# One of eight Wout pieces converted inside the last feed-forward instead of beside the experts

## The chip, the cores and the metric

The kernel runs on one core of one Trainium2 chip. The metric is the device time of one execution in microseconds (us). TensorE is written PE, VectorE DVE, ScalarE ACT, GpSimd POOL and the engine that issues most transfers SP.

## The reference, cut to what matters

```python
x = attention(q, k, v, bias from w1, b1, w2)      # 4 x 8 heads, 576 positions, 64 wide -> 2304 rows x 512
e = argmax(logits of 8 experts); gate = prob[e]   # per row
x = gate * (relu(x @ w1[e]) @ w2[e])              # 512 -> 1024 -> 512, one expert per row
h = x @ w_in                                      # 512 -> 2048
out = relu(h) ** 2 @ w_out                        # 2048 -> 512
```

`w_in` and `w_out` of the last feed-forward come as 64-bit floats. The kernel turns each into a pair of f16 tensors, a high part and the rest that it leaves, and forms a product as three f16 matmuls (high by high, high by rest, rest by high).

## The kernel before, in words

Three stages follow each other, and each overlaps the next at its edges.

**Attention and routing** fill the first 380 us. The change touches nothing there.

**The experts** follow. The rows are sorted into slots of 128 rows of one expert; `run_slots` (L1305) does 22 of them. A slot's PE work is `ff1` (L1222, 96 matmuls of 128 columns) and `ff2` (L1239, 24 matmuls of 512 columns), with a transposition of a later slot between. Where the expert changes, SP loads 2 MB of w1 (`load_slot`, into the tiles that the trace calls kst and wr) and four parts of 512 KB of already converted w2 (`load_w2`, L1019, `vt<-wsc` in the trace). The w2 parts of slot t+1 are asked for inside `ff2(t)`, each as soon as PE has finished with the part that it overwrites. SP issues in the order of the program and waits in that order.

Beside the experts the kernel converts the weights of the last feed-forward: eight pieces of Win, then eight pieces of Wout, 1 MB each (`convert`, L1112). One piece is: a load; on ACT the absolute value of the high words (L1127); on DVE a maximum, a shift with a mask and two bit operations that put a 32-bit float together (L1129 to L1134); for Wout four differences on POOL (L1147), since the last product is done with 7 block products out of 8; on ACT the high part (L1151); on DVE the rest (L1153); and, for Wout, a store of 896 KB to a scratch tensor `wosc` in DRAM (L1155). `pieces` (L1158) cuts all this into calls of a generator, 7 for each piece after the first two, so that neighbouring pieces interleave, and `piece(t, n)` (L1300) is called four times a slot (n = 0 after the first half of `ff1`, 1 before `ff2`, 2 and 3 right behind `ff2`). It advances the generator while fewer than 1 + (t - 2 + 0.25 n) * CPACE calls are done.

**The last feed-forward** (from L1394) goes over 9 blocks of 256 rows. First SP loads the eight Wout pieces back from `wosc` into `woh` (L1528). A block has eight units, `g_unit(j, c)` (L1425): 24 matmuls into a PSUM tile `pf` of which there are four; ACT applies relu into `gf` (L1440). At every odd c the square of the pair of units is taken (L1445 on ACT in blocks 0 and 1), POOL forms four sums (L1450), and `g_split` (L1454) then converts the pair *before* that one: a cast on ACT into the high part (L1457), a subtraction on DVE into the rest (L1458). There are two `gf` tiles, one for each pair in flight. The second matmul (`ff2_of`, L1461) is seven products of 24 matmuls (L1472). Each runs through the eight pieces c of `woh` in order, so piece 7 comes in the last three of the 24, and pair 3 of the block in the last six. The products of block j stand between the units of block j+1: from c = 5 on in block 1, from c = 3 on later. So 13 units run before the first product. `y_split` (L1414) makes f16 pairs of the next block's input rows in a tile `ysr` of its own (two of them), from which DMA transposes read.

Of the kernel before, what the change touches and what calls it, by code (L numbers as in the profile page):

```python
# [7 lines left out]
F32 = mybir.dt.float32  # L8
F16 = mybir.dt.float16
U32 = mybir.dt.uint32  # L10
I32 = mybir.dt.int32
AF = mybir.ActivationFunctionType
ALU = mybir.AluOpType
# [7 lines left out]
NT, DM = B * S, H * D  # L21
E, F1 = 8, 1024
F2 = 2048
P = 128
# [15 lines left out]
W1S, W2S, YS = 64.0, 64.0, 2.0 ** -8  # L40
WIS, RS, WOS = 64.0, 2.0 ** -8, 64.0
OUTS = 2.0 ** -22
CPACE = 6.1
NCONV, NWIN = 16, 8
HSW = 134
TINY64, HUGE = 2.0 ** -15 * 1.125, 3e38

# [37 lines left out]
def body(ctx: ExitStack, tc: tile.TileContext, q, k, v, wsm, emb, tau, mw1, mw2, win, wout, cst_d, lsk_d, ids_d, out):  # L85
    nc = tc.nc
    win, wout = win.bitcast(U32), wout.bitcast(U32)
    PE, ACT, DVE, POOL, SP = nc.tensor, nc.scalar, nc.vector, nc.gpsimd, nc.sync
# [18 lines left out]
    us_t = [cp.tile([P, XX], F32, name=f"us{i}") for i in range(4)]  # L107
# [850 lines left out]
    with tc.manual_schedule():  # L958
# [235 lines left out]
        wrp = ep("e_wr", 1)  # L1194
# [78 lines left out]
                DVE.tensor_copy(orow[:, i:i + 1], yr[:, DM + 1:XW])  # L1273


        conv = pieces([convert(i, wrp) for i in range(NCONV)])
        done = [0]
        state = ["tail"]
        yq, yd = [], []
# [115 lines left out]
        with ExitStack() as fctx:  # L1395
            fp = lambda n, bufs, **kw: tp(fctx, n, bufs, **(kw if "space" in kw else dict(side="right")))
            woh = fp("f_wo", 1).tile([P, 8, 2, 7, 256], F16, name="woh")
            gp = fp("f_g", 2)
            gfp = fp("f_gf", 2)
            op_ = fp("f_o", 2)  # L1400
            up = fp("f_u", 1)
            ysp2 = fp("f_ys", 2)
            pf1 = fp("f_p1", 4, space=PSUM)
            pf2 = fp("f_p2", 1, space=PSUM)
            NB = NTILE // 2
# [8 lines left out]
            def y_split(t):  # L1414
                y2, yr = yv(t // 2), us_t[t % 4]
                y_rows(t, yr)
                ysr = ysp2.tile([P, 2, 4, P], F16, name="ysr")
                y4 = yr[:, :DM].rearrange("p (k n) -> p k n", k=4)
                o = slice(t % 2 * P, t % 2 * P + P)
                ACT.copy(ysr[:, 0], y4)  # L1420
                DVE.tensor_tensor(out=ysr[:, 1], in0=y4, in1=ysr[:, 0], op=ALU.subtract)
                for a in range(2):
                    SP.dma_start_transpose(out=y2[:, a, :, o], in_=ysr[:, a].rearrange("p k n -> p (k n)"))

            def g_unit(j, c):  # L1425
                y2 = yv(j)
                if c == 0:
                    gts[j] = gp.tile([P, 2, 7, 8, P], F16, name="g2")
                p_ = pf1.tile([P, 2, 256], F32, name="pf1")
                for h in range(2):  # L1430
                    f, i = 8 * h + c, 0
                    for kc in range(4):
                        for a, b in ((0, 0), (0, 1), (1, 0)):
                            PE.matmul(p_[:, h], lhsT=wih[:, a, kc, f * P:(f + 1) * P], rhs=y2[:, b, kc, :],  # L1434
                                      start=(i == 0), stop=(i == 11))
                            i += 1
                if c % 2 == 0:
                    gfs[j] = gfp.tile([P, 8, 2, P], F32, name="gf")
                g = gfs[j]
                ACT.activation(g[:, 0:4, c % 2, :], p_.rearrange("p h (i n) -> p (h i) n", i=2), AF.Relu, scale=RS)  # L1440
                if c % 2 == 0:
                    return
                g4 = g[:, 0:4].rearrange("p q c n -> p (q c n)")
                if j < 2:
                    ACT.activation(g4, g4, AF.Square)  # L1445
                else:
                    DVE.tensor_tensor(out=g4, in0=g4, in1=g4, op=ALU.mult)  # L1447
                for d, x, y, op in ((4, 0, 2, ALU.add), (5, 4, 1, ALU.subtract), (6, 1, 0, ALU.subtract),
                                    (7, 3, 5, ALU.subtract)):
                    POOL.tensor_tensor(out=g[:, d], in0=g[:, x], in1=g[:, y], op=op)  # L1450
                g_split()
                late.append((g, gts[j], c - 1))

            def g_split():  # L1454
                while late:
                    g, gt, c = late.pop()
                    ACT.copy(gt[:, 0, :, c:c + 2, :], g[:, 1:8])  # L1457
                    DVE.tensor_tensor(out=gt[:, 1, :, c:c + 2, :], in0=g[:, 1:8], in1=gt[:, 0, :, c:c + 2, :], op=ALU.subtract)  # L1458

            def ff2_of(j):  # L1460
                gt = gts.pop(j)  # L1461
                m = [meta[:, 2 * j + i, 0:1] for i in range(2)]
                bank = [pf2.tile([P, 512], F32, name=f"pf2_{x}")[:, :256] for x in "abcd"]
                pa, pb, pc, pd = bank
                o = [op_.tile([P, DM], F32, name=f"o{i}") for i in range(2)]
                u = lambda nm: up.tile([P, 256], F32, name=nm)

                def prod(ps, s, w, first, end):
                    i = 0
                    for c in range(8):  # L1470
                        for a, b in ((0, 0), (0, 1), (1, 0)):
                            PE.matmul(ps, lhsT=gt[:, a, s, c, :], rhs=woh[:, c, b, w, :],  # L1472
                                      start=(i == 0 and first), stop=(i == 23 and end), skip_group_check=True)
                            i += 1

                def comb(dst, ps, i, x):
                    DVE.scalar_tensor_tensor(out=dst, in0=ps, scalar=m[i], in1=x, op0=ALU.mult, op1=ALU.add)  # L1477

                def put(i, ns=None):
                    t = 2 * j + i  # L1480
                    if t * P >= ZROW:
                        ch, b = TILES[t]
                        r0 = b * S + ch * P
                        for n in (0, 1) if ns is None else (ns,):
                            w = SP.dma_start(out=out[r0:r0 + P, 256 * n:256 * n + 256], in_=o[i][:, 256 * n:256 * n + 256]).ins
                            for other in outs:
                                tc.declare_no_dep(w, other, reason="disjoint rows")
                        return
                    if ns == 1:
                        return  # L1490
                    w = POOL.indirect_dma_start(out=out, out_offset=bass.IndirectOffsetOnAxis(ap=orow[:, t:t + 1], axis=0),
                                                in_=o[i], in_offset=None, bounds_check=NT - 1, oob_is_err=False).ins
                    for other in outs:
                        tc.declare_no_dep(w, other, reason="disjoint rows")
                    outs.append(w)

                prod(pa, 0, 0, True, False)
                s = [u(f"s{i}") for i in range(2)]
                for i in range(2):
                    ACT.activation(s[i], pa, AF.Copy, scale=m[i])  # L1500
                yield
                prod(pb, 4, 4, True, True)
                u2 = [u(f"u{i}") for i in range(2)]
                for i in range(2):
                    comb(u2[i], pb, i, s[i])
                yield
                prod(pc, 3, 3, True, False)
                u4 = u("u4")
                comb(u4, pc, 0, u2[0])
                yield  # L1510
                prod(pd, 5, 5, True, False)
                comb(o[0][:, 256:], pd, 0, u4)
                put(0, 1)
                yield
                prod(pa, 2, 2, False, True)
                ACT.activation(o[1][:, :256], pa, AF.Copy, scale=m[1])  # L1516
                yield
                prod(pc, 6, 1, False, True)
                comb(o[1][:, 256:], pc, 1, u2[1])
                put(1)  # L1520
                yield
                prod(pd, 1, 6, False, True)
                comb(o[0][:, :256], pd, 0, u2[0])
                put(0, 0)
                yield

            for g in range(8):
                SP.dma_start(out=woh[:, g].rearrange("p a q n -> p (a q n)"), in_=wosc[:, g * 3584:(g + 1) * 3584])  # L1528
            for j in range(NB):
                two = ff2_of(j - 1) if j else iter(())  # L1530
                last = j == NB - 1
                for c in range(8):
                    if c > (2 if j > 1 else 4) and not (last and c == 6):
                        next(two, None)
                    g_unit(j, c)
                    if 0 < j < NB - 1:
                        if c == 0:
                            y_load(j + 1)
                        if c in (3, 5):
                            y_split(2 * (j + 1) + c // 2 - 1)  # L1540
                if last:
                    g_split()
                for _ in two:
                    pass
# [68 lines left out]
```

## Time and profile before

| | us |
|---|---|
| median of 3 runs | 1004.47 (1001.83 to 1008.0) |
| the profiled execution | 1002.3 |
| its span, first to last instruction | 1000.4 |
| PE busy in the span | 946.6 (95%) |
| DVE / ACT / POOL busy | 665.8 / 541.6 / 502.7 |
| mean granted TensorE clock | 0.983 of full speed |

A time in the rows is in microseconds from the first instruction, unless it is marked ns. Busy shares are averages over stages with different limits, so the sections below read the stages one by one. "Idle before" is the time in which an engine stood still ahead of a group, with the event that ended most of it.

### The profile page before, as it was taken

The numbers are of one execution on the slowest core, as the hardware profiler recorded it, in microseconds if no ns is written. First come the engines' busy times: TensorE is split into PE (matmuls) and PEld (weight loads), VectorE is DVE, ScalarE is ACT, GpSimd is POOL, SyncE is SP. The second block draws the span as 40 slices with busy tenths as digits, with TensorE's granted clock in tenths as the row PEclk, the third lists the DMA queues.
The fourth block names the chain that finished last, engine by engine and source line by source line (L and its number), as shares of the span: only waits on it lengthen the run. The fifth ranks groups of instructions, "written<-read, shape, count | busy, mean of one in ns | idle before, by whom it ended". The sixth has DMA issues, their size and how long they took to land. (4 is left out here: it accounts for less than half of the span.)

```text
span 1000.4 us, 24973 instructions
## 1 busy us (share of the span) xinstructions
PE 946.6 (95%) x9725; PEld 750.8 (75%) x9725; DVE 665.8 (67%) x1260; ACT 541.6 (54%) x1000; POOL 502.7 (50%) x413
## 2 busy tenths in 40 slices
PE   8687999999899889999899999999999999999998
PEld 5355776677577668777667666688888888888887
DVE  6665999899998774687876987325455546364442
ACT  5576777777777574465665664355233324324231
POOL 1212537447434352466548787476455645454651
PEclk9799999999999989999999999999999999999999
DMA  8989885998779433698898574372111120111101
GB/s 292 318 244 298 292 290 196 277 273 294 222 250 335 155 129 120 236 336 309 330 407 320 196 294 159 119 315 43 33 54 34 36 59 17 49 44 32 33 1 43
DMA packets 79260, 187.18 MB, mean 187 GB/s; under 512 B 26680, under 2 KB 27320, under 8 KB 76544
## 3 DMA queue, kind: packets, MB, share of 16 engines
q1 hardware_dynamic: 73232, 170.50, 50.9%
q0 software_dynamic: 5904, 15.02, 4.4%
q8 instruction: 78, 1.28, 0.6%
q14 instruction: 46, 0.38, 0.1%
HBM read 171.65 MB, written 51.73 MB: 223 GB/s over the span
## 5 line engine op out<-in xcount | busy, mean ns | idle before, releaser
L1450 POOL TENSOR_TENSOR gf<-gf 128x256 f32<-128x256 f32 x144 | 166.1, 1173 | 144.2 <-DVE gf L1447 124.2
L1434 PE MATMUL pf<-big,wih 128*128 128x256 f16 x1728 | 196.0, 273 | 1.0 <-PEq L1388 1.0
L1434 PEld LDWEIGHTS <-wih 128*128 128x128 f16 x1728 | 169.0, 98 | 21.1 <-issue 1.5
L1472 PEld LDWEIGHTS <-g 128*128 128x128 f16 x1512 | 147.4, 98 | 18.7 <-issue 1.0
L1440 ACT ACTIVATE gf<-pf 128x512 f32<-128x512 f32 x72 | 42.3, 596 | 192.1 <-PE pf L1434 144.1
L1231 PE MATMUL ph<-x,w1b 128*128 128x128 f16 x2112 | 125.1, 219 | 2.9 <-ACT x L1215 1.7
L474 POOL TENSOR_TENSOR wh<-wr,w2s_c 128x1024 f16<-128x1024 f32 x32 | 62.3, 1946 | 127.9 <-DMA wr<-in_mw_dram 49.2
L1231 PEld LDWEIGHTS <-w1b 128*128 128x128 f16 x2112 | 120.6, 98 | 7.3 <-issue 1.9
L1246 PE MATMUL py<-vt,h 128*128 128x512 f16 x528 | 119.2, 383 | 5.0 <-DMA vt<-wsc 5.0
L525 ACT ACTIVATE pr<-ssb,mn 128x576 f32<-128x576 f32 x144 | 111.7, 776 | 10.3 <-DVE mn L512 10.2
L1458 DVE TENSOR_TENSOR g<-gf,g 128x1792 f16<-128x1792 f32 x36 | 85.2, 2367 | 46.0 <-ACT g L1457 46.0
L512 DVE CUSTOM_DVE_ANT_0 ssb<-ps_s,bias 128x576 f32<-128x576 f32 x144 | 107.5, 749 | 5.0 <-DMA bias<-bias_d 4.0
L1447 DVE TENSOR_TENSOR gf<-gf 128x1024 f32<-128x1024 f32 x28 | 34.3, 1225 | 114.2 <-ACT gf L1440 114.2
L501 PE MATMUL ps_s<-kst,qd 128*128 128x288 f16 (+1 forms) x640 | 97.1, 292 | 8.6 <-DVE mn L512 5.8
L1246 PEld LDWEIGHTS <-h 128*128 128x128 f16 x528 | 51.2, 99 | 64.0 <-issue 7.7
L534 PE MATMUL ps_t<-cst,pr 128*128 128x128 f32 x576 | 93.6, 286 | 1.4 <-DVE pt L212 1.1
L559 PE MATMUL pv<-pt,vt 128*64 128x128 f32 (+1 forms) x1280 | 85.0, 276 | 6.4 <-DMA vt<-in_v_dram 5.6
L559 PEld LDWEIGHTS pv<-pt,vt 128*64 128x64 f32 x1280 | 67.5, 141 | 22.9 <-issue 16.3
L534 PEld LDWEIGHTS ps_t<-cst,pr 128*128 128x128 f32 x576 | 65.9, 146 | 24.3 <-issue 18.2
L501 PEld LDWEIGHTS <-qd 128*128 128x128 f16 (+1 forms) x640 | 57.0, 102 | 23.6 <-issue 13.3
L1457 ACT CAST g<-gf 128x1792 f16<-128x1792 f32 x36 | 60.3, 1676 | 4.5 <-POOL gf L1450 4.4
L210 ACT COPY pt<-ps_t 128x512 f32<-128x512 f32 x99 | 57.1, 577 | 9.6 <-PE ps_t L534 9.3
(199 smaller groups left out, 1556.9 us busy)
## 6 DMA issues: line engine op xcount, KB each, us to landing
vt<-wsc SPq DMA_DIRECT2D x88, 512.0 KB
wr<-in_mw_dram SPq DMA_DIRECT2D x76, 512.0 KB
kst<-in_mw_dram SPq DMA_DIRECT2D x44, 512.0 KB
wsc<-wh SPq DMA_DIRECT2D x32, 512.0 KB
bias<-bias_d SPq DMA_DIRECT2D x16, 576.0 KB
bias_d<-rt SPq DMA_DIRECT2D x28, 295.5 KB
qd<-qh SPq DMA_DIRECT2D x64, 128.0 KB
wr<-in_win_dram SPq DMA_DIRECT2D x8, 1024.0 KB
```

What stands on the lines that cost most here:

```text
L474: POOL.tensor_tensor(out=wh[:, 0], in0=wr, in1=w2s_c.to_broadcast([P, 1024]), op=ALU.mult)
L501: PE.matmul(s[r, hf, :288], lhsT=qd[:, h2, i, pr, r], rhs=kst[x - x % 2][:, pr, h2, x % 2, js], start=(i == 0), stop=(i == 1))
L512: DVE.tensor_tensor_reduce(out=ss.rearrange("p (a j) -> p a j", a=2), in0=s[:, :, :288], in1=btile[bkey[u]][:, h2].rearrange("p (a j) -> p ...
L525: ACT.activation(pr_sb[k_ // 2][:, h2], ssb.pop(k_), AF.Exp, bias=mns.pop(k_), scale=-1.0, accum_out=sums[c, b][:, h:h + 1])
L534: PE.transpose(pt_ps[k_][:, jc * P:(jc + 1) * P], src[:, j0:j0 + P], eye)
L559: PE.matmul(pv[o, cs], lhsT=vb[:, 2 * jc + h2, d] if jc < 4 else vb[o, 8, d], rhs=a[h2][:, jc, cs] if jc < 4 else e[o, cs], start=(jc == 0 ...
L1231: PE.matmul(p_[:, f4, :], lhsT=w[:, a, kc, f * P:(f + 1) * P], rhs=x2[:, b, kc, :], start=(i == 0), stop=(i == 11))
L1246: PE.matmul(p_, lhsT=h2[:, a, fc, :], rhs=wb2[fc // 2][:, b, fc % 2, :], start=(i == 0), stop=(i == 23))
L1434: PE.matmul(p_[:, h], lhsT=wih[:, a, kc, f * P:(f + 1) * P], rhs=y2[:, b, kc, :], start=(i == 0), stop=(i == 11))
L1450: POOL.tensor_tensor(out=g[:, d], in0=g[:, x], in1=g[:, y], op=op)
L1458: DVE.tensor_tensor(out=gt[:, 1, :, c:c + 2, :], in0=g[:, 1:8], in1=gt[:, 0, :, c:c + 2, :], op=ALU.subtract)
L1472: PE.matmul(ps, lhsT=gt[:, a, s, c, :], rhs=woh[:, c, b, w, :], start=(i == 0 and first), stop=(i == 23 and end), skip_group_check=True)
```

## The change: one piece is left to the last feed-forward

Fifteen pieces are converted beside the experts in place of sixteen, and CPACE goes from 6.1 to 5.75 calls a slot, so that the fewer calls end at the same slot. The last piece (rows 7 of Wout) is loaded by SP at the start of the last feed-forward into a stretch of the second `g2` tile, which is empty until block 1 writes it. Its conversion is the generator `finish`, advanced by one step behind each of the units 3 to 9 (unit 8j + c): 3 the absolute value, 4 the two scalar operations, 5 and 6 the two bit operations, 7 four differences, on DVE now, 8 the high part, 9 the rest. It writes straight into `woh`, with no trip through DRAM. `gf` gets a third tile. The `ysr` tiles go: the f16 pair of input rows t is written over the row buffer that held rows t - 2. The `g2` tile is laid out by pairs.

```diff
-CPACE = 6.1
-NCONV, NWIN = 16, 8
+CPACE = 5.75
+NCONV, NWIN, NLATE = 16, 8, 1
...
-        conv = pieces([convert(i, wrp) for i in range(NCONV)])
+        conv = pieces([convert(i, wrp) for i in range(NCONV - NLATE)])
...
-            gfp = fp("f_gf", 2)
+            gfp = fp("f_gf", 3)
...
-            ysp2 = fp("f_ys", 2)
...
-                ysr = ysp2.tile([P, 2, 4, P], F16, name="ysr")
+                ysr = us_t[(t + 2) % 4][:, :DM].bitcast(F16).rearrange("p (a k n) -> p a k n", a=2, k=4)
...
-                if c == 0:
-                    gts[j] = gp.tile([P, 2, 7, 8, P], F16, name="g2")
+                if c == 0 and j not in gts:
+                    gts[j] = gp.tile([P, 4, 2, 7, 2, P], F16, name="g2")
...
+            for j in range(2):
+                gts[j] = gp.tile([P, 4, 2, 7, 2, P], F16, name="g2")
+            spare = gts[1].rearrange("p d a q c n -> p (d a q c n)").bitcast(U32)
+            rows = [spare[:, :2048], spare[:, 3072:5120]]
+            flat = spare[:, 5120:7168].bitcast(F32)
+            bits = [spare[:, 6144:7168], spare[:, 2048:3072]]
+            for i in range(NLATE):
+                g = 8 - NLATE + i
+                SP.dma_start(out=rows[i], in_=wout[g * P:(g + 1) * P, :])
+
+            def finish(i):
+                wr = rows[i].rearrange("p (n t) -> p n t", t=2)
+                lo, hi = wr[:, :, 0], wr[:, :, 1]
+                tb = flat.rearrange("p (q n) -> p q n", q=8)
+                af, b = flat[:, :1024], bits[i]
+                bf = b.bitcast(F32)
+                ACT.activation(bf, hi.bitcast(F32), AF.Abs)
+                yield
+                DVE.tensor_scalar(bf, bf, TINY64, None, op0=ALU.max)
+                DVE.tensor_scalar(b, b, 3, 0x3FFFFFF8, op0=ALU.logical_shift_left, op1=ALU.bitwise_and)
+                yield
+                DVE.scalar_tensor_tensor(out=b, in0=lo, scalar=29, in1=b, op0=ALU.logical_shift_right, op1=ALU.bitwise_or)
+                yield
+                DVE.scalar_tensor_tensor(out=af.bitcast(U32), in0=hi, scalar=0xC0000000, in1=b,
+                                         op0=ALU.bitwise_and, op1=ALU.bitwise_or)
+                yield
+                for d, x, y in ((4, 0, 1), (5, 2, 4), (6, 2, 0), (7, 3, 5)):
+                    DVE.tensor_tensor(out=tb[:, d], in0=tb[:, x], in1=tb[:, y], op=ALU.subtract)
+                yield
+                dh, dl = (woh[:, 8 - NLATE + i, a].rearrange("p q n -> p (q n)") for a in range(2))
+                ACT.activation(dh, flat[:, 256:], AF.Copy, scale=WOS)
+                yield
+                DVE.scalar_tensor_tensor(out=dl, in0=flat[:, 256:], scalar=WOS, in1=dh, op0=ALU.mult, op1=ALU.subtract)
+                yield
+
+            ends = [finish(i) for i in range(NLATE)]
+            ORDER = {u: (0,) for u in (3, 4, 5, 6, 7, 8, 9)}
+
-            for g in range(8):
+            for g in range(8 - NLATE):
                 SP.dma_start(out=woh[:, g]..., in_=wosc[:, g * 3584:(g + 1) * 3584])
...
                     g_unit(j, c)
+                    for i in ORDER.get(8 * j + c, ()):
+                        next(ends[i])
```

## Rows read from the trace of the kernel before

**Rows 1.** Busy time of each engine in two stretches, experts and last feed-forward.

```profile
core 0: us, PE busy (x) PEld busy (x) DVE busy (x) ACT busy (x) POOL busy (x), PEclk, DMA share, GB/s
380.00:642.00 262.00, 251.42 (x2897) 185.43 (x2898) 191.44 (x308) 146.08 (x186) 165.38 (x143) 0.99 0.72 264
642.00:997.00 355.00, 354.08 (x3240) 316.34 (x3240) 167.35 (x160) 126.67 (x158) 182.82 (x161) 1.00 0.19 60
```

**Rows 2.** Waits of PE from 380 to 642 us: total, times, longest.

```profile
PE py L1246 <- DMA vt<-wsc: 5.0, 3, 3.3
PE ph L1231 <- ACT x L1215: 1.7, 2, 1.0
PE ph L1231 <- DVE w1b L1026: 1.2, 2, 0.6
```

**Rows 3.** Timeline of PE: start, duration, work, count, idle before it and releaser.

```profile
477.79 7.03 PE L1246 MATMUL py<-vt,h 128*128 128x512 f16 x24 [3.32 <-DMA vt<-wsc]
...
490.46 5.34 PE L1246 MATMUL py<-vt,h 128*128 128x512 f16 x24
...
513.79 1.46 PE L1246 MATMUL py<-vt,h 128*128 128x512 f16 x6 [1.20 <-DMA vt<-wsc]
515.75 4.04 PE L1246 MATMUL py<-vt,h 128*128 128x512 f16 x18 [0.51 <-DMA vt<-wsc]
```

**Rows 4.** Timeline of SP: transfers that it issued, in its order.

```profile
460.61 0.34 SPq L1117 DMA_DIRECT2D wr<-in_win_dram  x1
462.56 3.02 SPq L1010 DMA_DIRECT2D kst<-in_mw_dram  x4
...
466.77 5.01 SPq L1019 DMA_DIRECT2D vt<-wsc  x4
...
500.57 0.37 SPq L1120 DMA_DIRECT2D wr<-in_wout_dram  x1
502.93 4.22 SPq L1019 DMA_DIRECT2D vt<-wsc  x4
```

**Rows 5.** Operations of a conversion, and nearest ones: duration ns least/median/most.

```profile
L1127 ACT ACTIVATE tb<-wr x16: 1131/1162/1197, 420.9 to 620.9; 128x1024 f32<-128x1024 f32 x16
L1129 DVE TENSOR_SCALAR tb<-tb x16: 678/684/1126, 422.7 to 625.1; 128x1024 f32<-128x1024 f32 x16
L1132 DVE SCALAR_TENSOR_TENSOR tb<-wr,tb x16: 1210/1222/2057, 424.4 to 626.5; 128x1024 uint32<-128x1024 uint32 x16
L1153 DVE SCALAR_TENSOR_TENSOR wr<-tb,wr x8: 2010/2014/2974, 553.6 to 641.9; 128x1792 f16<-128x1792 f32 x8
L1447 DVE TENSOR_TENSOR gf<-gf x28: 1224/1226/1226, 708.3 to 970.4; 128x1024 f32<-128x1024 f32 x28
```

**Rows 6.** Timeline of the start of the last feed-forward, all engines.

```profile
642.00 23.19 PE L1434 MATMUL pf<-big,wih 128*128 128x256 f16 x211 [1.04 <-PEq L1388]
...
648.06 1.08 ACT L1440 ACTIVATE gf<-pf 128x512 f32<-128x512 f32 x2 [5.75 <-SPq L1388]
...
651.55 4.08 SPq L1528 DMA_DIRECT2D woh<-wosc  x8
651.58 7.55 POOL L1450 TENSOR_TENSOR gf<-gf 128x256 f32<-128x256 f32 x8 [5.89 <-DMA y_d<-ys,yidx]
...
658.64 1.08 ACT L1440 ACTIVATE gf<-pf 128x512 f32<-128x512 f32 x2 [2.44 <-DVE g L1458]
...
660.89 4.68 POOL L1450 TENSOR_TENSOR gf<-gf 128x256 f32<-128x256 f32 x4 [1.76 <-ACT gf L1445]
...
672.65 1.06 ACT L1445 ACTIVATE gf<-gf 128x1024 f32<-128x1024 f32 x1
673.62 1.67 ACT L1457 CAST g<-gf 128x1792 f16<-128x1792 f32 x1
...
675.32 2.57 DVE L1458 TENSOR_TENSOR g<-gf,g 128x1792 f16<-128x1792 f32 x1 [3.87 <-ACT g L1457]
...
676.06 2.78 PE L1472 MATMUL pf_a<-woh,g 128*128 128x256 f16 x24
```

**Rows 7.** Stretches around the end of the loads of woh, columns as in rows 1.

```profile
655.00:672.00 17.00, 17.00 (x158) 15.25 (x156) 7.45 (x3) 9.11 (x10) 13.24 (x12) 1.00 1.01 415
672.00:676.00 4.00, 4.00 (x39) 3.58 (x38) 0.68 (x1) 3.25 (x4) 2.16 (x5) 1.00 0.04 13
```

More of the change, by code (lines that the diff above doesn't have):

```diff
@@ L1456, in g_split @@
                     g, gt, c = late.pop()
-                    ACT.copy(gt[:, 0, :, c:c + 2, :], g[:, 1:8])
-                    DVE.tensor_tensor(out=gt[:, 1, :, c:c + 2, :], in0=g[:, 1:8], in1=gt[:, 0, :, c:c + 2, :], op=ALU.subtract)
+                    ACT.copy(gt[:, c // 2, 0], g[:, 1:8])
+                    DVE.tensor_tensor(out=gt[:, c // 2, 1], in0=g[:, 1:8], in1=gt[:, c // 2, 0], op=ALU.subtract)
             def ff2_of(j):
@@ L1471, in prod @@
                         for a, b in ((0, 0), (0, 1), (1, 0)):
-                            PE.matmul(ps, lhsT=gt[:, a, s, c, :], rhs=woh[:, c, b, w, :],
+                            PE.matmul(ps, lhsT=gt[:, c // 2, a, s, c % 2, :], rhs=woh[:, c, b, w, :],
                                       start=(i == 0 and first), stop=(i == 23 and end), skip_group_check=True)
```

## The prediction

> **What bounds the kernel now.** I first read the busy time by stage. In the last feed-forward PE is busy for 354.08 of 355 us, at full granted clock; in the expert stage for 251.42 of 262 [rows 1]. So PE sets the time in both. Nothing that ACT, DVE or POOL are spared in the last stage can shorten it, and the change takes no matmul away. In the expert stage at most 262 - 251.42 = 10.6 us of idle PE can be won.
>
> Then I read who ends PE's idle time there: 5.0 us wait for converted w2, 1.7 for ACT and 1.2 for DVE [rows 2]. The 5.0 us are one wait of 3.32 us ahead of slot 7's second matmul and two, 1.20 + 0.51, at slot 10's [rows 3]. The first costs more than its idle time: the 24 matmuls behind it took 7.03 us where the same 24 took 5.34 later [rows 3], 1.7 us more. So transfers cost PE 5.0 + 1.7 = 6.7 us at most.
>
> SP's order says what those loads stand behind: slot 7's behind 1 MB of Win and 2 MB of w1, slot 10's behind 1 MB of Wout issued just ahead of it [rows 4].
>
> Last comes the start of the last stage, where the new work lands. Thirteen units run from 642.00 to 676.06, 2.62 us each, and the first product follows without idle time [rows 6].
>
> **Expert stage: the removed piece and the new pace.** A piece's load stands at a fixed call of the generator. Call m runs at the first point with (t - 2 + 0.25n) * CPACE over m - 2.
>
> The load issued at 500.57 is call 45. At 6.1 it is due at 43/6.1 = 7.05, so slot 9, n = 1, ahead of that slot's second matmul and of the w2 loads asked for inside it. At 5.75 it is due at 7.48, so n = 2, behind them. A megabyte at the 415 GB/s of a full queue [rows 7] is 2.5 us, more than the 1.71 us of slot 10's waits, so I let them go: **-1.7** (0 if something else is behind them, and no more than -1.7).
>
> The load issued at 460.61 is call 24: due at 22/6.1 = 3.61 before, (5, n = 3), and at 22/5.75 = 3.83 now, (6, n = 0). There it stands behind the 2 MB of w1 instead of ahead of it. Both stay ahead of slot 7's w2, so the bytes in front are the same. But SP no longer holds the w1 load back, which went out at 462.56, 2 us behind it [rows 4]. Its four issues may start up to 2 us earlier; I take **-1.3** of the 3.32 + 1.7 (ends 0 and -5.0: nearer 0, because the bytes ahead are unchanged).
>
> The rest of the missing piece (its ACT, DVE and POOL work, its 896 KB store) lies beside PE work. The waits for ACT and DVE, 2.9 us together, come from the order of the queues at a few moments, which the pace shifts; I take 0, with -2.9 and +3 as ends. Stage: **-3.0**.
>
> **Last feed-forward: finish.** Prices [rows 5, 6]: absolute value 1.16, two scalar operations 0.68 each (the second priced as the first), two bit operations 1.22 each, high part 1.67 (the cast of the same 1792 columns), rest 2.01. A difference of 256 columns on DVE is not shown. By the line through 1024 columns at 1.226 and 1792 at 2.014 it is 0.44; zero columns' share and a full 1.226 are the ends, so four cost 0.8 to 4.9, and I take 1.7, on the line. DVE gets 7.5 us more, ACT 2.8, POOL nothing, over units 3 to 9, 18.3 us.
>
> What counts is whether it is ready in time. Before, the wait for a free `gf` tile sets the pairs' rhythm (ACT idle 2.44 us until DVE's subtraction ended) [rows 6]. Relu 1.08, square 1.06, cast 1.67 and subtraction 2.57 follow one another, about 6.4 us for a pair against 5.24 on PE. Pair 3's subtraction ends at 675.32 + 2.57 = 677.89, and PE needs it at the 21st matmul of the first product, 676.06 + 20 * 0.109 = 678.24: 0.35 us of slack. The third tile takes that wait away; finish uses up the room again:
>
> - SP can issue the raw piece ahead of the eight loads of 651.55. At 415 GB/s it has landed by about 655.6 (2.5 us and, assumed, 1.5 until ACT may start). ACT is through with pair 0's cast at 658.64 - 2.44 = 656.2 [rows 6], so the absolute value ends at 657.4.
> - DVE: pair 0's subtraction from 656.2 to 658.8, scalar operations to 660.2; pair 1's subtraction to 663.9, the bit operations to 665.2 and 666.4; pair 2's to 669.1, the differences to 670.8.
> - ACT meets the high part right behind unit 8's relu, at 667.1, and stands there until 670.8. Queued behind it are unit 9's relu, pair 4's square and pair 3's cast. The high part ends at 672.5, pair 3's cast at 675.9.
> - DVE: pair 3's subtraction to 678.5, then the rest of piece 7 to 680.5. PE needs that at the 23rd matmul, 676.06 + 22 * 0.109 = 678.46. PE stands for **+2.0**.
>
> The ends: 0 if the differences take 0.8 and the subtractions 2.0 as on an idle DVE; +6 with bit operations at the longest 2.06, differences at 4.9 and a piece that lands 1.5 us later.
>
> Four POOL sums take 3.78 us before DVE works beside them and 4.68 when it does [rows 6]. DVE's two-input operations in finish, 6 us of them, can stretch POOL further, and pair 3's cast waits for POOL. At 6.2 us for four, the chain ends 1.0 us later; this is inside the +6.
>
> The Trainium skill, page "SBUF — State Buffer", section "Who interferes with whom", says that a DVE instruction with two SBUF inputs and a GpSimd instruction that reads SBUF exclude each other for the whole instruction. It speaks against moving the differences to DVE here, and the rows agree in direction (0.9 us more for four). By it alone the sum would be +3.0 for this step in place of +2.0.
>
> **Edits at nothing.** `woh` from seven loads in place of eight, with a raw megabyte ahead: 7.3 MB either way, and before they were in by 672 with nothing needed before 676 [rows 6, 7]. If that cover is gone, PE waits at its first product. `ysr` over the row buffers: the load of the next rows into the same buffer now waits on SP for the transposes that read it, with the next transposes queued behind; each has a block of 39 us (15 groups of 24 matmuls) and is needed only three units into it. The new layout of `g2` changes no operation.
>
> **Sum.** -1.7 - 1.3 + 2.0 = -1.0 on the profiled execution's 1002.3 gives 1001.3. That execution lies 2.2 below the median of the runs, 1004.47. I forecast **1002.5** for the median, half of that distance on top. Chance 0.55.
>
> **Rivals.**
>
> *The waits for w2 all go, and finish fits.* 1002.3 - 6.7 = 995.6. For: 15 pieces leave more room in a queue that was full around both places. Against: slot 7's load keeps 3 MB ahead of it. Chance 0.17.
>
> *Slower: the raw piece lands late.* Seven loads of 896 KB go out right behind it, and these filled the queue until 672 [rows 7]. If all share alike, the piece lands near 671. ACT stands at the absolute value with all relus behind it; PE has only four `pf` tiles, so unit 8, due at 662.96, starts after unit 4's relu at 672.75, 9.8 us late. The chain through finish then ends 6.9 us behind the product's need. 1002.3 - 3.0 + 16.7 = 1016.0. It decides from a landing later than about 661. Against: slot 10's first w2 part was in PE's use 1.96 us ahead of the next one [rows 3], as if transfers complete in order. Chance 0.06. The Trainium skill, page "DMA: Bandwidth & Descriptors", section "Queues, rings and completion order", says that descriptors of one ring are consumed in ring order, though completion is not promised in that order; by it this rival would be smaller still.
>
> *The expert stage only moves its waits.* No gain, another wait like slot 7's (3.3 + 1.7) at a load that now has a piece ahead of it, and +2.0: 1009.3. For: the queue is full there, and several loads change their place in it. Chance 0.14.
>
> *Nothing that PE sees changes*, because the third tile and the freed queues were hidden anyway and finish is in time: 1002.3. Chance 0.08.
>
> **Range and chances.** A measurement of this kernel can tell about 1% (10 us) from no change. The cases lie between 995.6 and 1009.3 but for the late piece; I give **995 to 1010**. Faster by over 1% (below 994.4) needs more than all w2 waits: 0.04. Slower by over 1% (above 1014.5) is the late piece: 0.05. Within: 0.91.
>
> **What would show it.** Right: slot 10's w2 wait gone, slot 7's shorter; units 0 to 12 without idle PE; PE idle some 2 us inside the first product, ended by DVE's rest of piece 7; ACT waiting some 4 us for the differences; no ACT wait for DVE's subtraction in block 0. Wrong: PE idle at unit 8 (the late piece), new w2 waits at other slots, or no idle PE in the first product.

## The result, and the profile after

The changed kernel takes 1018.45 us in the median against 1002.5 for the kernel before, a ratio of 1.0144 (95% interval 1.011 to 1.0177). I had forecast 1002.5 with a range to 1010: it came out slower than the range holds, and slower than before by 11.0 to 17.7 us.

A total alone misleads here. Slot 0's second matmul started anywhere between 395.2 and 414.1 us in the fourteen profiles of this study, though no kernel changes an instruction ahead of it. So I cut each profile at three points: the first `py` (slot 0's second matmul), the first `pf` (first unit) and the first `pf_a` and `pf_b` (first and second product).

| us | before | after | difference |
|---|---|---|---|
| start to slot 0's second matmul | 397.40 | 399.94 | +2.5, spread of the start |
| experts, to the first unit | 244.60 | 250.80 | **+6.2** |
| thirteen units, to the first product | 34.06 | 34.06 | 0 |
| first product, to the second | 5.24 | 10.83 | **+5.6** |
| the rest, to the end of the span | 319.10 | 319.27 | +0.2 |

The change lost 11.8 us of the profile's 14.5 in two places, and the interval of the runs holds that. PE's waits from 380 us to the first unit, as in [rows 2] (total, times, longest):

```profile
PE py L1246 <- DMA vt<-wsc: 4.7, 2, 3.0
PE ph L1231 <- ACT x L1215: 4.3, 3, 2.0
PE px L1214 <- POOL xs L1049: 3.5, 2, 3.0
```

And PE's timeline at these waits and at the first product, as in [rows 3] and [rows 6] (start, duration, work, count, idle before):

```profile
478.65 5.34 PE L1246 MATMUL py<-vt,h 128*128 128x512 f16 x24 [1.65 <-DMA vt<-wsc]
...
514.79 6.85 PE L1246 MATMUL py<-vt,h 128*128 128x512 f16 x24 [3.02 <-DMA vt<-wsc]
...
538.54 0.61 PE L1214 MATMUL px<-eye,xs 128*128 128x128 f16 x4 [3.02 <-POOL xs L1049]
538.95 4.20 PE L1231 MATMUL ph<-x,w1b 128*128 128x128 f16 x48
...
596.59 2.84 PE L1231 MATMUL ph<-x,w1b 128*128 128x128 f16 x48 [1.64 <-ACT x L1215]
...
609.75 4.47 PE L1231 MATMUL ph<-x,w1b 128*128 128x128 f16 x48 [2.01 <-ACT x L1215]
...
650.74 34.22 PE L1433 MATMUL pf<-big,wih 128*128 128x256 f16 x312 [1.51 <-PEq L1388]
684.80 2.35 PE L1471 MATMUL pf_a<-woh,g 128*128 128x256 f16 x20
688.67 0.39 PE L1471 MATMUL pf_a<-woh,g 128*128 128x256 f16 x2 [1.53 <-DVE g L1457]
691.13 0.38 PE L1471 MATMUL pf_a<-woh,g 128*128 128x256 f16 x2 [2.07 <-DVE woh L1558]
691.35 4.45 PE L1433 MATMUL pf<-big,wih 128*128 128x256 f16 x24
695.63 2.78 PE L1471 MATMUL pf_b<-woh,g 128*128 128x256 f16 x24
```

Read the durations beside the idle times. Each wait of 2 us and more here is followed by work that takes 1.4 to 1.7 us too long (6.85 for 5.34, 4.20 and 4.47 for 2.84, 4.45 for 2.78). The granted clock of those stretches says why (PEclk, third column from the right, a mean of full and half clock over the stretch):

```profile
core 0: us, PE busy (x) PEld busy (x) DVE busy (x) ACT busy (x) POOL busy (x), PEclk, DMA share, GB/s
514.80:521.50 6.70, 6.70 (x25) 2.75 (x25) 6.70 (x7) 3.01 (x5) 4.64 (x3) 0.77 1.02 413
539.00:543.00 4.00, 4.00 (x51) 4.00 (x49) 2.39 (x8) 1.73 (x2) 3.22 (x4) 0.65 0.97 386
609.80:614.00 4.20, 4.20 (x48) 4.20 (x48) 2.56 (x4) 1.60 (x3) 3.33 (x4) 0.59 0.68 277
688.60:695.60 7.00, 4.86 (x28) 3.59 (x29) 6.76 (x6) 3.43 (x5) 6.92 (x5) 0.76 0.10 19
```

The first product. Rows of DVE, ACT, POOL and SP there:

```profile
657.64 0.34 SPq L1534 DMA_DIRECT2D g<-in_wout_dram  x1
657.95 2.89 POOL L1449 TENSOR_TENSOR gf<-gf 128x256 f32<-128x256 f32 x4 [5.52 <-ACT gf L1444]
664.58 1.15 ACT L1542 ACTIVATE g<-g 128x1024 f32<-128x1024 f32 x1
668.42 12.09 POOL L1449 TENSOR_TENSOR gf<-gf 128x256 f32<-128x256 f32 x8 [0.55 <-ACT gf L1444]
678.11 3.02 DVE L1553 TENSOR_TENSOR g<-g 128x256 f32<-128x256 f32 x4
681.16 1.70 ACT L1556 ACTIVATE woh<-g 128x1792 f16<-128x1792 f32 x1 [4.53 <-DVE g L1553]
686.04 2.57 DVE L1457 TENSOR_TENSOR g<-gf,g 128x1792 f16<-128x1792 f32 x1 [4.91 <-ACT g L1456]
688.53 2.54 DVE L1558 SCALAR_TENSOR_TENSOR woh<-g,woh 128x1792 f16<-128x1792 f32 x1
```

ACT takes up the absolute value (664.58) without waiting for the raw piece, which SP had issued 6.9 us before. Later it stands 4.53 us for the differences; pair 3's subtraction and the rest of piece 7 come behind one another and end PE's two waits.

### The profile page after: what moved, and what is told of

The parts are those of the page before. It is cut to its first block, busy times and chain, and to the rows that moved or that the text cites. A ratio compares the mean times of both kernels' runs of the same rounds, so it can differ in the third digit from the quotient of the medians.

```text
span 1014.9 us, 24974 instructions
## 1 busy us (share of the span) xinstructions
PE 949.9 (94%) x9725; PEld 752.6 (74%) x9725; DVE 667.6 (66%) x1264; ACT 542.1 (53%) x1000; POOL 495.0 (49%) x409
## 5 line engine op out<-in xcount | busy, mean ns | idle before, releaser
L1449 POOL TENSOR_TENSOR gf<-gf 128x256 f32<-128x256 f32 x144 | 170.8, 1206 | 147.0 <-DVE gf L1446 124.3
L1231 PE MATMUL ph<-x,w1b 128*128 128x128 f16 x2112 | 127.7, 222 | 4.4 <-ACT x L1215 4.3
L1231 PEld LDWEIGHTS <-w1b 128*128 128x128 f16 x2112 | 123.5, 99 | 8.7 <-issue 3.5
```

The costliest lines, as they stand in the source:

```text
L1231: PE.matmul(p_[:, f4, :], lhsT=w[:, a, kc, f * P:(f + 1) * P], rhs=x2[:, b, kc, :], start=(i == 0), stop=(i == 11))
```

## The experiments

Where the loss comes from was cut first by place, then by cause. Stage lengths come from one profile each. The calls of before gave 244.60, 244.72 (e3) and 242.68 (e1), those of the changed kernel 250.80, 250.44 (e2) and 250.79 (e4), and one kernel profiled twice 240.18 and 238.89: a difference of less than 2 us says nothing. Each ratio is to runs of before that were taken beside it; their median was 1002.5 to 1012.5.

| | experts, us | first product, us | ratio to before (95%) |
|---|---|---|---|
| before | 244.60 | 5.24 | 1 |
| after | 250.80 | 10.83 | 1.0144 (1.011 to 1.0177) |
| e1 | 242.68 | 10.46 | 1.0041 (1.0015 to 1.0068) |
| e2 | 250.44 | 5.24 | 1.0039 (1.0002 to 1.0077) |
| e3 | 244.72 | 10.83 | 1.0038 (1.001 to 1.0067) |
| e4 | 250.79 | 5.28 | 1.0059 (1.0023 to 1.0094) |
| e5 | 245.61 | 5.28 | |
| e6 | 240.18 | 5.26 | |
| e7 | 245.34 | 5.28 | 0.999 (0.9963 to 1.0017) |
| e8 | 247.28 | 5.28 | 1.000 (0.9965 to 1.0036) |
| e9 | 238.89 | 5.27 | 0.9968 (0.9935 to 1.0002) |
| e10 | 240.54 | 5.25 | 0.9956 (0.9927 to 0.9985) |
| e11 | 249.29 | 5.24 | 1.0078 (1.0044 to 1.0112) |
| e12 | 239.14 | 5.26 | |

**e1, the last stage's edits alone.**

```diff
-CPACE = 5.75
+CPACE = 6.1
-        conv = pieces([convert(i, wrp) for i in range(NCONV - NLATE)])
+        conv = pieces([convert(i, wrp) for i in range(NCONV)])
```

> All sixteen pieces are converted beside the experts at 6.1 calls a slot, as before, and finish converts piece 7 a second time in the last feed-forward, with its own load and the third gf tile. Theory: the loss has two parts, about 6 us in the expert stage from where the calls fall at the pace of 5.75, and about 5.5 us at the first product of the last stage, where piece 7 comes late. Then this kernel has an expert stage like before (254 us from slot 0's second matmul at 397 to the first unit; within 2 us) and loses 5 to 6 us in the last stage: about 1008. Rival: the expert stage loses because of the edits to the last stage (another layout of its tiles). Then it is near 1016, with the expert stage 6 us longer here too.

The experts took 242.68, no longer than before, and the first product 10.46, with the same two waits of 1.55 and 2.07. The time was 1012.45, above the 1008 of the theory, but before itself stood at 1006.84 beside it; the ratio of 1.0041, or 1.5 to 6.8 us, agrees with -1.9 + 5.2 = 3.3 us. (The 254 us in the expectation is a slip: 642.0 - 397.4 is 244.6.) The new layout of the last stage costs the experts nothing.

**e2, the experts' part alone.**

```diff
-            for i in range(NLATE):
-                g = 8 - NLATE + i
-                SP.dma_start(out=rows[i], in_=wout[g * P:(g + 1) * P, :])
-            ORDER = {u: (0,) for u in (3, 4, 5, 6, 7, 8, 9)}
+            ORDER = {}
-            for g in range(8 - NLATE):
+            for g in range(8):   # piece 7 loaded from wosc's piece 6
```

> Fifteen pieces at 5.75 calls a slot and no finish; the conversion of piece 7 is left out, and woh's piece 7 is loaded from piece 6 in its place. Theory: the expert stage is 6 us longer than before with the same waits as in the changed kernel (x for ACT behind the high part, slot 10's w2, slot 12's xs), and the first product waits for nothing: about 1009. Rival: the expert stage's extra time is chance of that one profile: then 1000 to 1003.

250.44 and 5.24: the two losses are apart, and the expert stage's is no chance of one profile. The ratio, 0.2 to 7.8 us, holds the 5.8 of the stage. Slot 12's wait for xs was 5.1 us here where slots 7 and 10 waited 3.3 for w2 in place of 4.7: what PE gains at those loads it waits for later.

**e3, the pace alone.**

```diff
-CPACE = 5.75
+CPACE = 6.1
```

> The changed kernel with 6.1 calls a slot in place of 5.75, so each call of the fifteen pieces falls where it fell before and the end comes one slot sooner. Theory: the expert stage is like before or up to 2 us shorter, the first product of the last stage still waits 3 to 5 us with the slow clock behind it: 1005 to 1009. Rival: a missing piece costs whatever the pace (by lost spacing between transfers): 1013 to 1018.

244.72, with the waits of before one by one (3.24, 1.22 and 0.50 for w2, 1.04 for x). At this pace the missing piece neither costs nor wins anything that can be told, and the first product is as in the changed kernel. All of the +6.2 comes with the change of pace; whether by the pace itself or by where it puts the calls is for e6 to say. The time, 1009.33, lies just above the forecast, with before at 1006.84 beside it.

**e4, finish one unit shorter.**

```diff
-            ORDER = {u: (0,) for u in (3, 4, 5, 6, 7, 8, 9)}
+            ORDER = {3: (0,), 4: (0, 0), 5: (0,), 6: (0,), 7: (0,), 8: (0,)}
```

> The changed kernel with finish one unit shorter: the first bit operation goes to unit 4, and every later step one unit sooner, the rest of piece 7 at unit 8. Theory: ACT stands at the high part because DVE comes to the differences late; with the steps sooner pair 3's cast no longer waits behind it and piece 7 is ready before it is needed: the first product waits under 0.5 us, the clock stays at full, and the time falls by 4 to 5.5 us, to about 1013. Rival: DVE and POOL holding each other up set the end of the chain, and the order of the steps moves it by less than 1 us: 1017 to 1019.

The first product took 5.28, without a wait. In its timeline the high part and the rest of piece 7 are done 2 us before the product begins:

```profile
670.75 3.44 DVE L1553 TENSOR_TENSOR g<-g 128x256 f32<-128x256 f32 x4
674.11 2.01 DVE L1457 TENSOR_TENSOR g<-gf,g 128x1792 f16<-128x1792 f32 x1
674.22 1.70 ACT L1556 ACTIVATE woh<-g 128x1792 f16<-128x1792 f32 x1 [2.87 <-DVE g L1553]
676.05 2.01 DVE L1558 SCALAR_TENSOR_TENSOR woh<-g,woh 128x1792 f16<-128x1792 f32 x1
...
680.01 2.82 PE L1471 MATMUL pf_a<-woh,g 128*128 128x256 f16 x24
...
685.29 2.78 PE L1471 MATMUL pf_b<-woh,g 128*128 128x256 f16 x24
```

The differences now stand ahead of pair 2's subtraction on DVE (670.75 before 674.11), where in the changed kernel they came behind it (678.11). Counted from the first unit's start they begin 24.8 us after it in place of 27.4, and ACT's high part 28.3 in place of 30.4. The 5.6 us come from the order of finish, not from its work. Pair 3 has no room to spare: its subtraction ends at 682.17, and PE needs it, counted as in the prediction, at 682.19. All kernels below have this order but e11, which has no finish. By the ratios to before the order is worth more than that, 1.0059 against 1.0144, with wide intervals on both.

**e5, without POOL's differences beside the experts** (they are left out there).

```diff
-            for d, x, y, op in ((4, 0, 1, ALU.subtract), (5, 2, 4, ALU.subtract), (6, 2, 0, ALU.subtract),
-                                (7, 3, 5, ALU.subtract)):
-                POOL.tensor_tensor(out=tb[:, d], in0=tb[:, x], in1=tb[:, y], op=op)
```

> The changed kernel with finish one unit sooner, and the four POOL differences of the pieces beside the experts left out, so that ACT's high part there waits only for DVE. Theory: at 5.75 calls a slot ACT meets the high part ahead of the copy of x and stands behind POOL's differences, which is what PE waits for in slots 16 and 17 (1.64 and 2.01 us and a slow clock behind them). Then these waits fall below 1 us together and the expert stage comes down from 250.8 to 245 to 247, with slot 12's wait for xs unchanged, since no difference is formed before it. Rival: DVE's conversions beside the splits of x and w1 are what makes ACT and POOL late: the waits stay within 1 us of 3.65 and the stage at 249 or more.

The stage fell from 250.79 to 245.61, inside the theory's bounds, and PE's waits for x in slots 16 and 17 are gone (a wait for x is counted to the slot in which x is copied; PE stands at the start of the next). The 1.0 that is left lies ahead of slot 0. Slot 12's wait for xs, expected unchanged at 3.0, was 4.7; other profiles of this schedule have 5.1 (e2) and 4.8 (e4).

```profile
PE px L1211 <- POOL xs L1049: 4.7, 1, 4.7
PE py L1243 <- DMA vt<-wsc: 2.4, 2, 1.4
...
PE ph L1228 <- ACT x L1212: 1.0, 1, 1.0
```

In the changed kernel the chain reads: DVE's last bit operation, POOL's differences (behind a scatter that POOL issues from 587.93 to 589.35), ACT's high part, and only then the copy of x.

```profile
586.39 1.33 DVE L1134 SCALAR_TENSOR_TENSOR tb<-wr,tb 128x1024 uint32<-128x1024 uint32 x1 [0.96 <-DVEq L1035]
...
589.38 2.91 POOL L1147 TENSOR_TENSOR tb<-tb 128x256 f32<-128x256 f32 x4
...
592.32 1.70 ACT L1151 ACTIVATE wr<-tb 128x1792 f16<-128x1792 f32 x1 [5.75 <-POOL tb L1147]
...
595.52 1.01 ACT L1215 COPY x<-px 128x1024 f16<-128x1024 f16 x1
```

ACT stands 5.75 us ahead of 592.32 with the relu and the copy of x queued behind. What e5 also takes away is POOL's 2.9 us a piece, so it does not tell ACT's queue from POOL's load. These rows show the chain through ACT's queue; a kernel that only puts the high part behind the copy of x was not run.

**e6, two calls in advance at the same pace.**

```diff
-            while done[0] < (1 if t < 2 else 1 + (t - 2 + 0.25 * n) * CPACE):
+            while done[0] < (1 if t < 2 else 3 + (t - 2 + 0.25 * n) * CPACE):
```

> The changed kernel with finish one unit sooner, still at 5.75 calls a slot, with two calls done in advance: the same work and spacing, each call falls about a third of a slot earlier. Theory: it is the place where a call falls, not the pace or the fewer pieces, that costs 6 us: the waits change place and the expert stage moves by 2 us or more from 250.8, either way. Rival: the pace itself is bad: 250 to 251.5 with waits of the same kind and sum.

240.18: 10.6 us shorter than at the same pace without the advance, and 4.4 shorter than before. So neither the slower pace nor the fewer pieces need cost anything: the 6.2 us depend on where the calls fall.

**e7 and e8, y rows read back early**, at 6.1 and at 5.75.

```diff
-                    if t == 9:
-                        for n in range(4):
-                            SP.dma_start(out=us_t[n][:, :XW], in_=y_d[n * P:(n + 1) * P, :])
+                    if 2 <= t < 6:
+                        SP.dma_start(out=us_t[t - 2][:, :XW], in_=y_d[(t - 2) * P:(t - 1) * P, :])
```

> Fifteen pieces at 6.1 calls a slot, finish one unit sooner, and the first four blocks of y rows read back in slots 2 to 5, one a slot, in place of all four in slot 9. Theory: POOL's scatter of slot 10's rows must wait until the four loads of slot 9 have landed, and they go out into a full queue; that holds POOL for 9.4 us and makes xs late in slot 12. With the loads in slots 2 to 5, where the queue has room, POOL's wait is gone, 1 MB less stands ahead of w2 in slots 10 and 11, and the expert stage falls below 244.6, by 1 to 3 us; the first product takes 5.24. Total 1 to 3 us below before. Rival: POOL's wait is for something else and w2's waits are set by the bytes before slot 9: 244 to 245, total equal to before.

> The same at 5.75 calls a slot. Theory: slot 12's wait for xs (3.02 us in the changed kernel, with 1.4 of slow clock behind it) goes, those for ACT in slots 16 and 17 stay: expert stage 246 to 248. Rival: slot 12's wait comes from DVE conversions beside POOL's work at this pace: 249.5 to 251, with that wait within 1 us of what it was.

In e7 POOL's wait (9.43 us in the changed kernel, 9.25 in the kernel before) ahead of slot 10's scatter was gone (0.17 left), and slot 12's wait with it. But the stage was 245.34, where I expected less than 244.6: the w2 waits stayed at 4.9 us and ran at the slow clock. The theory of POOL's wait held, that of the gain fell, and the time equals that of before, as the rival had it. In e8 slot 12's wait went, the stage fell by 3.5 to 247.28, and the waits for x stayed at slots 16 and 17 (1.64 and 2.03), as the theory had it.

**e9 and e10, the better version.** e9 is the kernel of e6, timed; e10 adds the early y rows.

> The kernel of e6 again (fifteen pieces, 5.75 calls a slot, two calls in advance, finish one unit sooner), timed in rounds against before. Theory: its expert stage of 240.2 against 244.6 repeats within 1 us, the first product takes 5.2, and it is 0.3 to 0.6% faster than before. Rival: that profile was a lucky one: stage 243 or more, no difference that can be measured.

> The kernel of e9 with the first four blocks of y rows read back in slots 2 to 5. Theory: slot 12's last 1.35 us of waiting for xs go and nothing comes in their place: stage 238.5 to 240, 0.4 to 0.7% faster than before. Rival: loads taken from slot 9 come to stand ahead of w2 in slots 5 to 7, and the waits for w2 grow by what slot 12 saves: 240 to 242.

e9's stage came out at 238.89, 1.3 below e6's where I expected 1 at most. Its time is lower by 0.3%, but its interval just touches no change. e10 beats before by 0.44%, interval 0.15 to 0.73%; its stage of 240.54 lies in the rival's range. Slot 12 no longer waits, but slot 10 waits 3.64 us for w2 and its 24 matmuls take 8.16 in place of 5.34, more than what slot 12 saved. So the early rows add nothing that these runs can tell from e9. PE's waits in e9, where nothing is left from slot 13 on:

```profile
PE py L1246 <- DMA vt<-wsc: 4.2, 3, 2.2
PE px L1214 <- POOL xs L1049: 1.6, 1, 1.6
PE ph L1231 <- ACT x L1215: 0.7, 1, 0.7
```

**e11, the advance without the change.** The line of e6, in the kernel before.

> The kernel before (sixteen pieces at 6.1, all beside the experts) with two calls in advance, as in e6. Theory: what e6 wins comes from where the calls fall and is to be had without moving a piece: the expert stage changes by 2 us or more from 244.6, and if it falls to 241 the moved piece is worth nothing. Rival: the room that fifteen pieces leave is what lets e6 pass slots 13 to 21 without a wait of PE: 243.5 to 245.5 here.

249.29: it moved by more than 2 us, as the theory allows and the rival does not, but upward. What e6 wins is not to be had by the advance alone; two calls that help fifteen pieces at 5.75 hurt sixteen at 6.1, with waits for x and xs all along the stage:

```profile
PE ph L1231 <- ACT x L1215: 4.6, 4, 1.9
PE py L1246 <- DMA vt<-wsc: 4.3, 2, 3.4
PE px L1214 <- POOL xs L1049: 3.8, 4, 1.6
```

**e12, four calls in advance.** The line of e6 with 5 in place of 3.

> The kernel of e6 with four calls in advance in place of two. Theory: the stage depends on where ACT's high part and DVE's conversions fall between PE's needs, so it lies anywhere between 239 and 251, with waits at other slots than at two. Rival: the earlier the calls, the better: 240 or less.

239.14, with small waits at other places (xs 0.79 and 0.97 us late in the stage). It lies in the range of both theories, so it decides nothing alone; with e6 it shows that two calls are not a single lucky spot. Whether sixteen pieces have such a spot too was not tried beyond e11, so it is not shown that moving the piece is what makes e9 and e10 faster than before.

## Why the prediction was wrong

**What bounds the kernel** was right. PE sets the time, the thirteen units took 34.06 us to the hundredth, the rest of the last stage moved by 0.2, and everything lost is idle PE and the clock behind it.

**The step that failed** is the expert stage, -3.0 as forecast and +6.2 as measured. Of its three terms:

- *Slot 7's w2, -1.3.* Right in direction: the wait fell from 3.32 to 1.65 and the 24 matmuls behind it took 5.34 instead of 7.03 [rows 3], together -3.4. With the same calls it was 1.09 in e2 and 1.07 in e4. How large the gain is, one profile does not settle: e1, with the calls of before, had 2.16 and no slow clock.
- *Slot 10's w2, -1.7, "so I let them go".* They did not go: 1.71 became 3.02 with 1.5 of slow clock, and 2.2 in e2 and e4. I followed the one load that moved behind slot 10's w2 and overlooked the load before it, which moved as well: call 38, due at 36/6.1 = 5.90 before, so (8, n = 0), and at 36/5.75 = 6.26 after, so (8, n = 2). Before, that piece went out at 490.7; now it stands at 495.65, and a megabyte is ahead of slot 10's w2 after all:

```profile
492.79 2.76 SPq L1019 DMA_DIRECT2D vt<-wsc  x4
495.65 0.37 SPq L1120 DMA_DIRECT2D wr<-in_wout_dram  x1
497.64 2.64 SPq L1010 DMA_DIRECT2D wr<-in_mw_dram  x4
502.11 4.26 SPq L1019 DMA_DIRECT2D vt<-wsc  x4
508.32 0.34 SPq L1120 DMA_DIRECT2D wr<-in_wout_dram  x1
```

  That this load is what keeps the wait is not shown. In e1 both loads are where they were before, in e6 calls 38 and 45 are back at (8, n = 0) and (9, n = 1), and slot 10 waits in both. What sets this wait stays open. Slot 10's second matmul in e1, then in e6:

```profile
514.47 6.86 PE L1246 MATMUL py<-vt,h 128*128 128x512 f16 x24 [3.04 <-DMA vt<-wsc]
```

```profile
517.18 5.34 PE L1246 MATMUL py<-vt,h 128*128 128x512 f16 x24 [2.69 <-DMA vt<-wsc]
```

- *The waits for ACT, DVE and POOL, "I take 0, with -2.9 and +3 as ends".* This is the term that decided. Slot 12's wait for xs went from 0.70 to 3.02, with 1.4 of slow clock; those behind it from 2.67 to 4.16, with 1.6 of slow clock. Together about +6.8. I had seen that the pace shifts the order of the queues and then priced the shift at nothing, without following a Wout piece's calls into the slots. Behind slot 12 there was an order to work out: ACT's high part is the third call after POOL's differences, and where the two fall so that the copy of x is queued behind, PE waits (shown by e5 and the rows beside it).

  Slot 12's wait is not all new. POOL's scatter of slot 10's rows is held for the y rows in both kernels, and xs comes a few POOL operations behind it. Before, then after:

```profile
526.95 1.58 POOL L1264 DMA_INDIRECT y_d<-ys,yidx  x1 [9.25 <-DMA wr<-in_mw_dram]
...
532.86 1.47 POOL L1049 TENSOR_TENSOR xs<-xg,xs 128x512 f16<-128x512 f32 x1
```

```profile
529.68 1.08 POOL L1264 DMA_INDIRECT y_d<-ys,yidx  x1 [9.43 <-DMA wr<-in_mw_dram]
...
536.42 2.07 POOL L1049 TENSOR_TENSOR xs<-xg,xs 128x512 f16<-128x512 f32 x1
```

  Counted from slot 0's second matmul, xs is ready 1.6 us later after the change, and PE comes for it 0.7 sooner. The scatter itself is only 0.2 later; POOL's operations behind it took longer, beside other DVE operations than before. That these stretch them is argued, not shown.

  The single waits up to slot 12 trade places from profile to profile, their sum does not. With the slow clock behind them, slots 7, 10 and 12 lost 7.4, 7.4 and 6.7 us with the calls of before (before, e3, e1) and 10.6, 10.4 and 10.3 with those of the change (after, e2, e4). So about half of the +6.2 was lost up to slot 12, and half behind it.

  A wait of about 2 us was followed in several places by 1.4 to 1.7 more at the slow clock. I had that row for slot 7 and used it only as a gain.

**The first product** went as told, step by step. The high part was to end at 672.5, 30.5 us after the first unit's start, and ended at 682.86, 32.1 after; PE waited for pair 3 and then for the rest of piece 7. Only the size was off, +5.6 for +2.0, inside that term's end of +6: four differences took 3.02 where I put 1.7, the scalar operations 1.22 and 1.24 for 0.68 each, the bit operations 1.75 and 1.63 for 1.22 each, eight POOL sums 12.09 where I put 4.68 for four, so pair 3's cast and subtraction came later too, 3.6 us of wait in all; the 1.7 of slow clock behind it I had not priced.

My 3.78 for four POOL sums "before DVE works beside them" was a misreading: it is the mean of eight, and DVE's subtraction runs beside the last of them. Beside an idle DVE four took 2.89 in the changed kernel (657.95), so DVE's work cost POOL more than I read. The 1.5 us that I assumed before ACT may start on the raw piece is in no row; the piece was there when ACT came to it. The Trainium skill, page "SBUF — State Buffer", section "Who interferes with whom", has DVE's two-input operations and POOL's reads shut each other out; these rows agree in direction, since both took longer side by side, and the +3.0 that I gave by it was nearer than my +2.0.

**The edits at nothing** were right: e1 and e3 show no cost of the layout, the seven loads or the third tile outside the first product.

**The rivals.** The slow one came near the measured time by another way: the raw piece was not late and unit 8 did not wait. "The expert stage only moves its waits", 1009.3, had the mechanism, and I gave it 0.14 with one new wait where there were several. The sum of its kind, +6.2 + 5.6 on 1002.3, is 1014.1; to the profile's 1016.65 the later start of the experts adds 2.5, and the median lies 1.8 above the profile.

## What to carry to other kernels

Work that is dealt out beside a bound engine by a pace has a phase as well: write down, for each piece, the point at which every one of its calls falls before and after, loads and waits on other engines alike, before a change of pace is priced. Changing the phase alone moved the stage from 250.8 to 240.2 us here, more than three times the 3.0 that I had forecast for the stage. Where an in-order engine feeds the bound one, keep what waits for a slow third engine behind the feed, and count the slow clock that can follow a wait of about 2 us. The first half of this advice is argued from e5 and the rows beside it; no kernel here was reordered so.

## What the runs showed of the hardware that I had not expected

Idle PE of 1.65 us in one piece left the next 24 matmuls at 5.34 us; 3.02 us was followed by a granted clock of 0.77 in the next 6.7 us, 2.01 by 0.59 in the next 4.2. Waits of 2.16 in e1, 2.21 in e2 and 2.69 in e6 were followed by 24 matmuls in 5.34, one of 1.95 in e7 by 24 in 7.04, so the length of one wait does not settle it; what else does stays open. Four POOL sums of 256 columns took 2.89 us with an idle DVE, 4.69 beside one subtraction of 1792 columns and 6.0 beside the conversion, and DVE's own subtraction of 256 columns 0.75 us where the line through longer ones gave 0.44.
